# One exp over two score units, one PSUM bank for each pair of heads, three query buffers, and a new order of the steps

## The chip, the cores and the metric

The kernel runs on one core of one Trainium2 chip. Times are device microseconds of one execution; the time that counts is the median over several executions. Engines are named as in the profile: PE is TensorE (matmuls; PEld its weight loads), DVE is VectorE, ACT is ScalarE, POOL is GpSimd, SP is SyncE, which here issues nearly all DMAs.

## What is computed

The reference is attention with a soft cap on the scores, followed by a Fourier mixing block and a feed-forward block, all in fp32. Batch 4, 12 heads, 448 tokens, head size 64, so the model width is 768 and the hidden width 3072.

```python
scores = cap * np.tanh((q @ k.T / 8) / cap)
attn = exp(scores - max); attn = attn / (sum(attn) + 1e-9)
x = attn @ v                                   # heads side by side: (4, 448, 768)
u = x + real(fft(fft(x, axis=1), axis=2))
un = (u - mean(u)) / sqrt(var(u) + 1e-6)       # over the 768 features
out = u + relu(un @ w_ch1) @ w_ch2
```

## The kernel before, in words

**Attention.** The 48 heads are taken as 24 pairs, and two pairs make a group of four heads with 14 weighing units (numbered u) in 7 score units (numbered t, 84 in all, two weighing units each). A weighing unit is a tile of 128 keys of one head against all 448 queries; since 448 is three and a half tiles, the last 64 keys of heads share a tile, the unit in the middle of a group. `scores(t)` (L402) makes eight matmul instructions on 64x64 quadrants of PE into a PSUM tile `s` of two banks (two such tiles); `tanh(t)` (L418) reads them into an SBUF tile `a` of 2 x 448 columns (five such tiles), and `exp(t)` (L422) works on that tile in place. `weigh(u)` (L428) multiplies the weights with V, to which a column of ones is attached, so that the sums of the softmax come out as one more column; it accumulates a pair of heads in one PSUM tile `av` of two banks, one head in each bank, and there is one such tile (`bufs=1`). When a pair is complete, `denominators(p)` (L459) and `normalise(p)` (L469) on DVE read it: an add of the guard, a reciprocal, a memset and four multiplications (L477) into `u`, the tile of one batch.

**Mixing.** For each batch DVE folds tokens and features (L496, L502, L511 to L515), PE makes two stages of matmuls (`stage1` L533, `stage2` L561), ACT and DVE combine between them (L549, L553), DVE adds to `u` (L581, L585), takes mean and variance, and standardises (L637; on ACT for the last batch, L635). PE transposes the result (`u_cols` L644) and ACT copies it into the accumulator `xc`. `operand` and `operand_rest` split it into a leading fp32r part and a rest; `residual` (L768) scales and adds a row of `dev` or `mean`.

**Feed-forward.** 12 groups of two hidden tiles; for each batch `up` (L770) makes 36 matmuls of 128x448 into `ph`, ACT takes the relu (L789), DVE its rest (L790), and `down` (L793) makes 36 matmuls, six in each of six PSUM groups, which DVE adds to `xc` (L821). Groups with an odd `dc` use a bank of the tag `d`; those with an even one use bank 0 or 1 of a two-bank tile of the tag `av`, which is taken anew where `dc` is a multiple of 4. In the first of the 12 groups `down_first` (L828) fills the first two PSUM groups side by side, by hidden tile, adds both (L845), and hands on its two-bank tile, so that `dc` = 2 goes on in bank 1 of it. The fp64 weights are split on DVE and ACT: a half chunk is one `fetch` and three `weights` steps of nine operations (L693 to L725).

**What sets the order.** Nothing is scheduled by a compiler: `ORDER` gives each step a place by hand, the steps are sorted by it, and each engine takes its instructions strictly in that order. An engine whose next instruction waits for a semaphore holds all that stands behind it, and so does SP with its DMAs. `needs` only asserts that the order is possible. All steps up to the last `tanh` run with two `s` tiles; after it their four banks become `ph` banks, so no feed-forward matmul can come before the last `tanh`. PSUM has eight banks: `s` four (later `ph`), `av` two, `d` two.

Of the kernel before, what the change touches and what calls it, by code (L numbers as in the profile page):

```python
# [19 lines left out]
P = 128  # L20
# [38 lines left out]
GF = 2  # L59

# [5 lines left out]
PAD = 16, 16  # L66
# [24 lines left out]
    [(("q", 4), ("q", 4))] * 2 + [(("k", 3), ("k", 3))] + ["x1"] * 3,  # L91
# [10 lines left out]
        268, 267, 275, 302, 488, 487, 523, 524, 710, 727, 693, 702, 841, 846, 843, 850  # L102
    ],
    "combine": [
        237, 243, 238, 249, 436, 437, 449, 452, 649, 670, 659, 673, 830, 832, 826, 831
    ],
    "denominators": [
        44, 75, 104, 124, 155, 187, 216, 248, 286, 319, 342, 378, 426, 465, 504, 534, 566, 594, 641,
        686, 717, 748, 776, 793
    ],  # L110
    "exp": [
# [5 lines left out]
    ],  # L117
    "fetch": [
        8, 32, 43, 79, 145, 222, 299, 388, 479, 834, 854, 893, 921, 948
    ],  # L120
    "fold_features": [
        214, 228, 210, 223, 415, 419, 395, 407, 629, 637, 627, 634, 813, 815, 809, 811
    ],
    "fold_tokens": [
        149, 168, 186, 164, 196, 194, 261, 287, 367, 336, 382, 386, 498, 592, 554, 557, 607, 608, 698,
        749, 775, 767, 803, 804
    ],
    "guards": [
        6
    ],  # L130
    "load_constant": [
        133, 110, 66, 212
    ],
    "load_k": [
        0, 28, 50, 37, 91, 106, 128, 161, 177, 245, 258, 264, 315, 376, 372, 438, 494, 477, 515, 581,
        590, 650, 699, 737
    ],
    "load_q": [
        1, 15, 11, 25, 49, 59, 80, 76, 115, 152, 165, 176, 202, 213, 234, 280, 262, 308, 334, 348, 359,
        397, 402, 433, 490, 503, 502, 548, 539, 570, 632, 666, 646, 704, 725, 736  # L140
    ],
    "load_v": [
# [3 lines left out]
    ],  # L146
    "mirror": [
        199, 203, 387, 393, 609, 619, 805, 806
    ],
    "moments": [  # L150
        273, 312, 307, 311, 495, 510, 544, 532, 729, 733, 759, 762, 852, 855, 853, 856
    ],
    "normalise": [
        46, 82, 109, 127, 157, 190, 219, 251, 290, 321, 343, 381, 431, 470, 514, 541, 569, 600, 647,
        690, 722, 751, 777, 798
    ],
    "operand": [
        421, 425, 453, 454, 442, 507, 695, 639, 677, 715, 678, 799, 848, 816, 828, 900, 901, 906, 909,
        923, 916, 907, 920, 927
    ],  # L160
    "operand_rest": [
        458, 430, 486, 469, 456, 537, 720, 652, 680, 723, 763, 833, 886, 822, 887, 902, 910, 911, 912,
        929, 925, 938, 937, 941
    ],
    "product": [
# [3 lines left out]
    ],  # L169
    "residual": [  # L170
        605, 642, 800, 837, 866, 897, 932, 919, 934, 956, 953, 963
    ],
    "row": [
        584, 752, 908, 946
    ],
    "rows": [
        341, 561, 783, 867
    ],
    "rows_cols": [
        346, 564, 794, 875  # L180
    ],
    "rows_copy": [
        355, 598, 795, 880
    ],
    "rows_out": [
        405, 418, 466, 416, 621, 661, 657, 675, 810, 861, 840, 851, 888, 922, 928, 939
    ],
    "scales": [
        4
    ],  # L190
    "scores": [
# [5 lines left out]
    ],  # L197
    "stage1": [
        233, 242, 236, 246, 434, 435, 443, 446, 640, 658, 651, 664, 827, 829, 824, 821
    ],  # L200
    "stage2": [
        259, 254, 269, 291, 473, 472, 505, 511, 709, 716, 684, 687, 838, 845, 839, 849
    ],
    "standardise": [
        363, 354, 347, 368, 567, 576, 583, 580, 790, 789, 791, 786, 876, 879, 883, 874
    ],
    "tanh": [
# [17 lines left out]
    "weigh": [
# [9 lines left out]
    ],  # L235
# [44 lines left out]
def attention_fft_ffn(  # L280
# [63 lines left out]
    nc.gpsimd.memset(vt[:, :, :, :1], 1.0)  # L344
# [77 lines left out]
    def exp(t):  # L422
        nc.scalar.activation(a_t[t], a_t[t], AF.Exp, scale=capt)  # L423
# [643 lines left out]
```

## Time and profile before

| | us |
|---|---|
| three runs | 910.24, 911.3, 913.85 (median 911.3) |
| the profiled execution | 913.63 |
| its span, first to last instruction | 910.8 |
| PE busy in the span | 892.0 |
| DVE busy | 728.4 |
| ACT busy | 327.1 |
| first and last `av` matmul | 10.7 and 195.8 |

The granted clock of PE is at its full level in the whole span. The page is one execution as the hardware profiler took it. A busy time is the share of a stretch that the instructions of an engine cover; PE's matmuls overlap and their ends are modelled, so a busy PE can still have slack inside. Behind a group of instructions the page gives the idle time just before them and what ended it. The chain of waits goes back from the last instruction, at each step to what released it.

### The profile page before, as it was taken

How to read it: one execution, taken by the hardware profiler on the slowest of the kernel's cores; microseconds unless marked ns; L12 is line 12 of the kernel's file. 1: busy time of each engine (PE TensorE's matmuls, PEld its weight loads, DVE VectorE, ACT ScalarE, POOL GpSimd, SP SyncE). 2: the span in 40 equal slices, each digit the busy share in tenths (PEclk: the TensorE clock that was granted, in tenths of full speed). 3: DMA queues.
4: the chain of work that ended last, by engine and by line, in shares of the span. 5: the costliest groups of instructions: out<-in, count | busy, mean ns of one | idle time of the engine just before them, and what ended most of it. 6: DMA issues, size and time to landing. Idle time of an engine off the chain costs nothing.

```text
span 910.8 us, 17992 instructions
## 1 busy us (share of the span) xinstructions
PE 892.0 (98%) x7452; PEld 784.8 (86%) x7452; DVE 728.4 (80%) x1540; ACT 327.1 (36%) x503; POOL 9.7 (1%) x19
## 2 busy tenths in 40 slices
PE   8899999999989999999999999999999999999998
PEld 4566676778889999999999999999999999999998
DVE  4689999999889787878878788787787877878633
ACT  7989999961502212122221221212212221222200
POOL 0000001000000000000000000000000000000000
PEclk9999999999999999999999999999999999999999
DMA  7653535210202121211212211111211111221033
GB/s 212 172 139 104 135 91 164 66 47 1 74 4 84 53 63 55 72 59 53 63 53 63 65 57 53 53 53 53 67 57 53 53 52 53 54 68 53 18 120 123
DMA packets 50465, 66.60 MB, mean 73 GB/s; under 512 B 25408, under 2 KB 36560, under 8 KB 50384
## 3 DMA queue, kind: packets, MB, share of 16 engines
q1 hardware_dynamic: 50096, 65.13, 24.6%
q8 instruction: 58, 0.95, 0.4%
q10 hardware_dynamic: 288, 0.33, 0.1%
q14 instruction: 23, 0.19, 0.1%
HBM read 59.92 MB, written 5.52 MB: 72 GB/s over the span
## 4 chain that ended last, share of the span: by engine, by line
PE 90%; DVE 7%; issue 1%; ACT 1%; POOL 0%; DVEq 0%; POOLq 0%
PE po L813 37%; PE ph L778 37%; PE av L439 7%; PE s L410 6%; PE pq L561 2%; DVE u L477 1%; PE yps L533 1%; DVE xc L768 1%; DVE tf L502 1%; DVE tf L496 1%; DVE ff L515 0%; DVE y L553 0%; PE warm L351 0%; DVE xs L329 0%; PE pt L644 0%
## 5 line engine op out<-in xcount | busy, mean ns | idle before, releaser
L778 PE MATMUL ph<-xs,w 128*128 128x448 f32 x1728 | 353.3, 362 | 0.0
L813 PE MATMUL po<-hh,w 128*128 128x448 f32 (+1 forms) x1686 | 343.7, 362 | 3.6 <-DVE xc L845 3.6
L778 PEld LDWEIGHTS ph<-xs,w 128*128 128x128 f32 x1728 | 323.4, 187 | 21.9 <-issue 0.3
L813 PEld LDWEIGHTS po<-hh,w 128*128 128x128 f32 x1686 | 314.3, 187 | 27.1 <-DVE xc L845 5.1
L821 DVE TENSOR_TENSOR xc<-xc,po 128x448 f32<-128x448 f32 (+1 forms) x281 | 172.2, 616 | 40.3 <-PE po L813 40.2
L790 DVE SCALAR_TENSOR_TENSOR hh<-ph,hh 128x448 fp32r<-128x448 f32 x96 | 59.9, 624 | 87.3 <-ACT hh L789 86.6
L691 ACT ACTIVATE wt<-raw 128x384 f32<-128x384 f32 x84 | 46.6, 555 | 230.5 <-DVE w L725 230.5
L789 ACT ACTIVATE hh<-ph 128x448 fp32r<-128x448 f32 x96 | 52.3, 544 | 187.1 <-PE ph L778 187.1
L439 PEld LDWEIGHTS av<-vt,a 128*64 128x64 f32 (+1 forms) x2688 | 76.7, 137 | 33.7 <-issue 17.2
L439 PE MATMUL av<-vt,a 128*64 128x65 f32 (+1 forms) x2688 | 82.5, 223 | 8.0 <-issue 3.7
L420 ACT ACTIVATE a<-s,tscale 128x896 f32<-128x896 f32 x84 | 82.5, 1005 | 11.8 <-PE s L410 9.7
L324 ACT CAST w<-wt 128x384 fp32r<-128x384 f32 x84 | 42.8, 510 | 117.8 <-DVE wt L700 117.8
L423 ACT ACTIVATE a<-a,capt 128x896 f32<-128x896 f32 x84 | 83.6, 1039 | 0.4
L410 PE MATMUL s<-q,k 64*64 64x448 f32 x672 | 78.5, 560 | 1.5 <-ACT a L420 1.5
L700 DVE SCALAR_TENSOR_TENSOR wt<-wt 128x384 f32<-128x384 f32 x96 | 53.6, 558 | 9.2
L697 DVE SCALAR_TENSOR_TENSOR wt<-raw,wt 128x384 uint32<-128x384 uint32 x96 | 53.7, 559 | 3.3
L725 DVE TENSOR_TENSOR w<-wt 128x384 fp32r<-128x384 f32 x96 | 53.6, 558 | 3.3
L719 DVE SCALAR_TENSOR_TENSOR wt<-raw,wt 128x384 f32<-128x384 uint32 x96 | 53.5, 557 | 2.9
L329 DVE TENSOR_TENSOR wt<-wt,w 128x384 f32<-128x384 f32 x96 | 52.8, 550 | 0.0
L410 PEld LDWEIGHTS s<-q,k 64*64 64x64 f32 x672 | 23.0, 134 | 21.4 <-issue 9.6
L694 DVE TENSOR_SCALAR wt<-raw 128x384 uint32<-128x384 uint32 x96 | 34.1, 355 | 1.1
L716 DVE TENSOR_SCALAR wt<-wt 128x384 uint32<-128x384 uint32 x96 | 33.9, 354 | 0.5
(65 smaller groups left out, 367.7 us busy)
## 6 DMA issues: line engine op xcount, KB each, us to landing
raw<-w2r SPq DMA_DIRECT2D x48, 384.0 KB
raw<-w1r SPq DMA_DIRECT2D x48, 384.0 KB
q<-qr SPq DMA_DIRECT2D x35, 224.5 KB
outT<-xc SPq DMA_DIRECT2D x23, 224.0 KB
k<-kr SPq DMA_DIRECT2D x12, 256.0 KB
vt<-vr SPq DMA_DIRECT2D x24, 128.0 KB
vt<-vr SPq DMA_DIRECT2D x24, 96.0 KB
k<-kr SPq DMA_DIRECT2D x12, 192.0 KB
```

Of the source, the lines that this page charges most:

```text
L410: nc.tensor.matmul(ps_t[t][h * D : (h + 1) * D, n, :SQ], kt[q, k][rows, k0, h], qk[q, x][rows, :SQ], start=True, stop=True,)
L420: nc.scalar.activation(a_t[t], ps_t.pop(t)[:, :, :SQ], AF.Tanh, scale=tscale)
L423: nc.scalar.activation(a_t[t], a_t[t], AF.Exp, scale=capt)
L439: nc.tensor.matmul(pa_t[p][half * D : (half + 1) * D, j, g * (D + 1) : g * (D + 1) + w], a_t[t][rows, n, q : q + D], vt[rows, p % 2].rearr ...
L697: nc.vector.scalar_tensor_tensor(tu, hi.bitcast(U32), 0xC0000000, tu, op0=ALU.bitwise_and, op1=ALU.bitwise_or)
L700: nc.vector.scalar_tensor_tensor(t, w, HI_MIN, t, op0=ALU.is_ge, op1=mul)
L719: nc.vector.scalar_tensor_tensor(w, lo, 2.0**-52, w, op0=mul, op1=mul)
L725: nc.vector.tensor_tensor(ws[c][1][:, sl], t, w, op=add)
L778: nc.tensor.matmul(ph[:, :S], w_[:, dc * P : (dc + 1) * P], x_, start=(k_ == 0), stop=(k_ == 3 * NDC - 1),)
L790: nc.vector.scalar_tensor_tensor(hh[:, 1], ph[:, :S], 0.0, f32(hh[:, 0]), op0=ALU.max, op1=sub)
L813: nc.tensor.matmul(po[:, q0:q1], w_[:, dc * P : (dc + 1) * P], hh[:, x_, q0:q1], start=(k_ == 0), stop=(k_ == 3 * GF - 1),)
L821: nc.vector.tensor_tensor(ac[:, q0:q1], ac[:, q0:q1], po[:, q0:q1], op=add)
```

## The change

Two score units of `tanh` go into the two halves of one `a` tile of 4 x 448 columns, and one `exp` works on all of it; there are three such tiles instead of five of half the size, and the feed-forward's `hh` uses them likewise, one for a batch. Each pair of heads gets a PSUM tile `av` of one bank, with its seven blocks of 65 columns behind one another, and two such tiles take turns. The tail units in the middle of a group now hold one head of each pair, not two heads of one pair, so that pair p + 1 is begun (its bank taken) one unit before pair p ends. The column of ones stands behind V, not in front. The q of a group comes in two loads instead of three, into three buffers instead of four. In the feed-forward even `dc` take the one-bank `av` tiles in turn. `yh` has one buffer, the padding is larger, loads of V wait for fewer units, and all of `ORDER` is new: 917 steps instead of 971 (42 exps and 12 q loads fewer). The host lays out q, k and v accordingly. The core of the diff, with the lists of `ORDER` cut:

```diff
+ABUFS = 3
...
-PAD = 16, 16
+PAD = 24, 16
...
-    [(("q", 4), ("q", 4))] * 2 + [(("k", 3), ("k", 3))] + ["x1"] * 3,
+    [(("q", 3), ("q", 3)), (("q", 3), ("k", 3)), (("k", 3), ("k", 3))] + ["x1"] * 3,
...
     "exp": [
-        16, 17, 26, 31, 38, 56, 61, 69, 74, 85, 92, 107, 108, 111, 126, 130, 138, 140, 150, 162, 171,
...
+        19, 31, 55, 63, 84, 88, 108, 117, 132, 143, 158, 176, 192, 200, 231, 257, 264, 278, 298, 310,
...
     "tanh": [
-        7, 12, 18, 21, 33, 35, 48, 57, 54, 71, 73, 89, 93, 103, 120, 123, 131, 132, 146, 159, 147, 160,
...
-        735, 758, 772, 764, 781
+        8, 9, 16, 21, 22, 37, 43, 58, 62, 71, 73, 86, 87, 97, 103, 111, 113, 124, 125, 138, 142, 155,
...
+        690, 691, 708, 710, 718
     ],
...
     "weights": [
-        9, 24, 27, 40, 67, 84, 87, 96, 97, 113, 122, 141, 180, 230, 235, 326, 349, 380, 422, 444, 445,
-        556, 586, 648, 663, 689, 825, 872, 878, 894, 915, 930, 940, 944, 947, 950, 959, 962, 964, 966,
-        968, 970
+        36, 38, 39, 41, 49, 54, 65, 70, 78, 92, 106, 116, 134, 160, 162, 208, 226, 241, 341, 394, 405,
+        413, 558, 610, 624, 779, 802, 825, 833, 860, 871, 885, 889, 895, 901, 906, 907, 909, 911, 912,
+        915, 916
     ],
...
     "residual": [
-        605, 642, 800, 837, 866, 897, 932, 919, 934, 956, 953, 963
+        588, 645, 539, 706, 816, 849, 872, 862, 881, 899, 892, 903
...
-    nc.gpsimd.memset(vt[:, :, :, :1], 1.0)
+    nc.gpsimd.memset(vt[:, :, :, D:], 1.0)
...
-        qk[q, i] = new([P, SQ + 1], F32, "q", 4, "q")
-        (nc.scalar if q == 0 and i == 0 else nc.sync).dma_start(qk[q, i], qr[q, i])
+        qk[q, i] = new([P, SQ + 1], F32, "q", 3, "q")
+        (nc.scalar if q == 0 and i == 0 else nc.sync).dma_start(qk[q, i], qr[q, i // 2])
...
-        nc.sync.dma_start(vt[:, p % 2, n0:n1, 1:], vr[p // NP, PAIRS[p % NP], :, n0:n1])
+        nc.sync.dma_start(vt[:, p % 2, n0:n1, :D], vr[p // NP, p % NP, :, n0:n1])
...
-                x = (2 * n if n == h else 1) if i == 3 else 2 * (i > 3)
+                x = 2 * (h if i == 3 else i > 3)
...
-        a_t[t] = new([P, 2, SQ], F32, "a", 5, "a")
-        nc.scalar.activation(a_t[t], ps_t.pop(t)[:, :, :SQ], AF.Tanh, scale=tscale)
-
-    def exp(t):
-        nc.scalar.activation(a_t[t], a_t[t], AF.Exp, scale=capt)
+        if t % 2 == 0:
+            a_t[t // 2] = new([P, 4, SQ], F32, "a", ABUFS, "a")
+        nc.scalar.activation(a_t[t // 2][:, t % 2 * 2 : t % 2 * 2 + 2], ps_t.pop(t)[:, :, :SQ], AF.Tanh, scale=tscale)
+
+    def exp(m):
+        nc.scalar.activation(a_t[m], a_t[m], AF.Exp, scale=capt)
...
     def weigh(u):
         t, n = divmod(u, 2)
         p, head, c = chunk(u)
-        if u % NC == 0:
-            pa_t[p] = psum.tile([P, 2, 512], F32, tag="av", bufs=1, name="av")
-        i = 6 if head is None else 2 * c + head
-        first, last = ((0, 1), (6, 6)) if p % 2 == 0 else ((0, 0), (6, 6))
-
-        def tile(j, g, half, rows, n, i):
+        if u % (2 * NC) in (0, NC - 1):
+            pa_t[u // NC + (u % NC > 0)] = psum.tile([P, 512], F32, tag="av", name="av")
+
+        def tile(p, j, g, half, rows, n, i, start):
+            block = 3 * j + g if g < 3 else 6
             q = (2 * g + half) * D if g < 3 else 6 * D
-            w = D + 1 + int(g == 2 and c == 0 and half != j)
             nc.tensor.matmul(
-                pa_t[p][half * D : (half + 1) * D, j, g * (D + 1) : g * (D + 1) + w],
-                a_t[t][rows, n, q : q + D],
-                vt[rows, p % 2].rearrange("k n c -> k (n c)")[:, i * (D + 1) : i * (D + 1) + w],
-                start=u % NC == first[j] and g == 0,
-                stop=u % NC == last[j] and g == 3,
+                pa_t[p][half * D : (half + 1) * D, block * (D + 1) : (block + 1) * (D + 1)],
+                a_t[t // 2][rows, t % 2 * 2 + n, q : q + D],
+                vt[rows, n if i == NC - 1 else p % 2, i],
+                start=start,
+                stop=False,
                 skip_group_check=True,
             )
 
+        if head is None:
+            p -= p % 2
+            for g in range(3):
+                for h in range(2):
+                    for half in range(2):
+                        tile(p + h, n, g, half, slice(h * D, (h + 1) * D), n, NC - 1, h == 1 and n == g == 0)
+            if n == 1:
+                for j in range(2):
+                    for h in range(2):
+                        tile(p + h, j, 3, j, slice(h * D, (h + 1) * D), j, NC - 1, False)
+            return
         for g in range(3):
-            for j in (0, 1) if head is None else (head,):
-                rows = slice(P) if head is not None else slice(j * D, (j + 1) * D)
-                for half in range(2):
-                    tile(j, g, half, rows, n, i)
-        for j in range(2):
-            if head is None:
-                tile(j, 3, j, slice(j * D, (j + 1) * D), n, i)
-            elif head == 1:
-                tile(j, 3, j, slice(P), n - 1 + j, i - 1 + j)
+            for half in range(2):
+                tile(p, head, g, half, slice(P), n, 2 * c + head, u % (2 * NC) == g == 0)
+        if head == 1:
+            for j in range(2):
+                tile(p, j, 3, j, slice(P), n - 1 + j, 2 * c + j, False)
 
     def denominators(p):
         b = p // NP
         if b not in u_t:
             u_t[b] = new([P, 4, DM], F32, f"x{b % 2}", 1, "u")
             nc.gpsimd.memset(u_t[b][FOLD:, 3], 0.0)
-        pa = pa_t[p][:, :, : 4 * (D + 1)].rearrange("q j (g c) -> q j g c", g=4)
-        den = den_t[p] = new([P, 2, 4, 1], F32, "den", 2, "den")
-        nc.vector.tensor_scalar_add(den, pa[:, :, :, :1], guard)
+        pa = pa_t[p][:, : 7 * (D + 1)].rearrange("q (i c) -> q i c", i=7)
+        den = den_t[p] = new([P, 7, 1], F32, "den", 2, "den")
+        nc.vector.tensor_scalar_add(den, pa[:, :, D:], guard)
         nc.vector.reciprocal(den, den)
 
     def normalise(p):
         b, c0 = p // NP, PAIRS[p % NP] * 2 * D
-        pa = pa_t[p][:, :, : 4 * (D + 1)].rearrange("q j (g c) -> q j g c", g=4)[..., 1:]
+        pa = pa_t[p][:, : 7 * (D + 1)].rearrange("q (i c) -> q i c", i=7)[:, :, :D]
         den = den_t[p]
         u = u_t[b][:, :, c0 : c0 + 2 * D].rearrange("q g (j c) -> q j g c", j=2)
 
-        def part(out, rows, j, g):
-            x = pa[rows, j, g]
-            nc.vector.tensor_tensor(out, x, den[rows, j, g].to_broadcast(x.shape), op=mul)
-
-        part(u[D:FOLD, :, 3], slice(FOLD, P), slice(2), 2)
-        nc.vector.memset(den[FOLD:, :, 2], 0.0)
+        def part(out, rows, i):
+            x = pa[rows, i]
+            nc.vector.tensor_tensor(out, x, den[rows, i].to_broadcast(x.shape), op=mul)
+
+        part(u[D:FOLD, :, 3], slice(FOLD, P), slice(2, 6, 3))
+        nc.vector.memset(den[FOLD:, 2:6:3], 0.0)
         for j in range(2):
-            part(u[:D, j, 3], slice(j * D, (j + 1) * D), j, 3)
-        part(u[:, :, :3], slice(P), slice(2), slice(3))
+            part(u[:D, j, 3], slice(j * D, (j + 1) * D), 6)
+        nc.vector.tensor_tensor(
+            u[:, :, :3],
+            pa[:, :6].rearrange("q (j g) c -> q j g c", j=2),
+            den[:, :6].rearrange("q (j g) c -> q j g c", j=2).to_broadcast([P, 2, 3, D]),
+            op=mul,
+        )
...
-        half = new([P, 2, NK], F32, "yh", 2, "yh")[:FW]
+        half = new([P, 2, NK], F32, "yh", 1, "yh")[:FW]
...
-            hh = hs[b, n] = new([P, 2, S], F32R, "a", 5, "hh")
+            if n == 0:
+                hs[b] = new([P, GF, 2, S], F32R, "a", ABUFS, "hh")
+            hh = hs[b][:, n]
...
-            if dc % 2:
-                po = psum.tile([P, 512], F32, tag="d", name="po")
-            else:
-                if dc % 4 == 0:
-                    both = psum.tile([P, 2, 512], F32, tag="av", bufs=1, name="po")
-                po = both[:, dc % 4 // 2]
+            po = psum.tile([P, 512], F32, tag=("av", "d")[dc % 2], name="po")
...
-        both = psum.tile([P, 2, 512], F32, tag="av", bufs=1, name="po")
-        po = both[:, 0], psum.tile([P, 512], F32, tag="d", name="po")
+        po = [psum.tile([P, 512], F32, tag=tag, name="po") for tag in ("av", "d")]
...
-            at(load_v, p, i, needs=[("weigh", u) for u in units(p - 2)])
+            at(load_v, p, i, needs=[("weigh", 7 * p - 8 + n) for n in range(2 - p % 2)] if p > 1 else [])
...
-        at(tanh, t, needs=[("scores", t), ("scales",)])
-        at(exp, t, needs=[("tanh", t)])
+        at(tanh, t, needs=[("scores", t), ("scales",)] + [("tanh", t - 1)] * (t % 2))
+        if t % 2:
+            at(exp, t // 2, needs=[("tanh", t - 1), ("tanh", t)])
...
-                at(denominators, p, needs=[("weigh", 7 * p + 6), ("guards",)] + ([("denominators", p - 1)] if p else []))
+                at(denominators, p, needs=[("weigh", 7 * p + 7 - p % 2), ("guards",)] + ([("denominators", p - 1)] if p else []))
...
```

## Rows read from the trace of the kernel before

**Rows 1.** The page: busy time of PE, and the chain that ended last by engine.
```profile
PE 892.0 (98%) x7452; PEld 784.8 (86%) x7452; DVE 728.4 (80%) x1540; ACT 327.1 (36%) x503; POOL 9.7 (1%) x19
...
PE 90%; DVE 7%; issue 1%; ACT 1%; POOL 0%; DVEq 0%; POOLq 0%
```
**Rows 2.** Stretches: busy PE, PEld, DVE, ACT, POOL (instructions), clock, DMA share, GB/s.
```profile
20.00:40.00 20.00, 17.75 (x381) 11.08 (x375) 13.34 (x40) 19.03 (x21) 0.00 (x0) 1.00 0.52 139
40.00:60.00 20.00, 18.02 (x415) 12.49 (x414) 12.93 (x32) 17.01 (x20) 0.00 (x0) 1.00 0.58 164
60.00:80.00 20.00, 19.46 (x408) 14.73 (x404) 18.08 (x48) 16.51 (x21) 0.00 (x0) 1.00 0.32 91
...
120.00:140.00 20.00, 19.57 (x414) 13.69 (x416) 19.17 (x51) 19.19 (x21) 0.70 (x1) 1.00 0.40 106
...
190.00:200.00 10.00, 8.62 (x179) 7.25 (x172) 9.20 (x29) 6.40 (x9) 0.79 (x1) 1.00 0.19 49
...
220.00:300.00 80.00, 77.03 (x402) 70.26 (x399) 71.45 (x148) 23.50 (x44) 1.27 (x2) 1.00 0.17 49
300.00:600.00 300.00, 300.00 (x1501) 280.94 (x1500) 247.10 (x474) 63.95 (x125) 0.00 (x0) 1.00 0.20 58
```
**Rows 3.** The tile av: its matmuls, ns min/median/max, first and last start in us.
```profile
L439 PE MATMUL av<-vt,a x2688: 213/222/272, 10.7 to 195.8; 128*64 128x65 f32 x144, 64*64 64x65 f32 x48
```
**Rows 4.** The chain in order of time: start, us, what.
```profile
34.24 3.32 PE av L439 x112
...
37.59 0.24 DVE den L466
...
39.02 0.57 DVE u L477
...
39.84 1.04 PE av L439 x28
40.88 1.66 PE s L410 x16
```
**Rows 5.** Who waited for whom: us in total, times, longest.
```profile
PEld av L439 <- DVE u L477: 4.0, 5, 0.9
...
PE po L813 <- DVE xc L845: 3.6, 4, 1.4
...
PE av L439 <- DVE u L477: 1.8, 3, 0.6
```
**Rows 6.** The page's groups: busy, mean ns of one, idle before and what ended it.
```profile
L420 ACT ACTIVATE a<-s,tscale 128x896 f32<-128x896 f32 x84 | 82.5, 1005 | 11.8 <-PE s L410 9.7
...
L423 ACT ACTIVATE a<-a,capt 128x896 f32<-128x896 f32 x84 | 83.6, 1039 | 0.4
...
L700 DVE SCALAR_TENSOR_TENSOR wt<-wt 128x384 f32<-128x384 f32 x96 | 53.6, 558 | 9.2
...
L694 DVE TENSOR_SCALAR wt<-raw 128x384 uint32<-128x384 uint32 x96 | 34.1, 355 | 1.1
```
**Rows 7.** Timeline around the third batch's first down groups: start, us, what, idle before.
```profile
250.33 2.08 DVE L768 TENSOR_TENSOR xc<-xc,dev 128x896 f32<-128x896 f32 x2
252.33 1.14 DVE L845 TENSOR_TENSOR xc<-xc,po 128x448 f32<-128x448 f32 x2
253.00 3.28 PE L813 MATMUL po<-hh,w 128*128 128x448 f32 x15 [1.43 <-DVE xc L845]
```
**Rows 8.** Timeline of ACT from 40 us.
```profile
40.32 1.97 ACT L423 ACTIVATE a<-a,capt 128x896 f32<-128x896 f32 x2
```
**Rows 9.** Groups by form in 0:230: two copies by ACT of different lengths.
```profile
L324 ACT COPY xc<-pt 128x448 f32<-128x448 f32 x17 | 9.1, 548 | 2.7 <-PE pt L644 2.7
...
L324 ACT COPY yh<-yps 97x256 f32<-97x256 f32 x16 | 5.9, 375 | 8.4 <-PE yps L533 6.4 <-DVE y L553 1.7 <-ACT a L423 0.2
```
**Rows 10.** Timeline of the start.
```profile
9.64 1.96 ACT L423 ACTIVATE a<-a,capt 128x896 f32<-128x896 f32 x2
...
10.72 1.50 PE L439 MATMUL av<-vt,a 128*64 128x65 f32 x40
```

More of the change, by code (lines that the diff above doesn't have):

```diff
@@ L109 @@
-        686, 717, 748, 776, 793
+        51, 74, 101, 133, 152, 172, 217, 230, 280, 305, 331, 354, 411, 438, 476, 498, 542, 552, 609,
+        631, 676, 704, 730, 742
     ],
     "exp": [
[5 rows of a table removed]
+        19, 31, 55, 63, 84, 88, 108, 117, 132, 143, 158, 176, 192, 200, 231, 257, 264, 278, 298, 310,
+        325, 342, 363, 402, 427, 446, 453, 471, 489, 508, 519, 537, 553, 579, 604, 630, 655, 675, 683,
+        698, 711, 721
     ],
     "fetch": [
-        8, 32, 43, 79, 145, 222, 299, 388, 479, 834, 854, 893, 921, 948
+        5, 30, 48, 76, 107, 147, 295, 313, 532, 761, 811, 886, 896, 904
@@ L120 @@
     ],
     "fold_features": [
-        214, 228, 210, 223, 415, 419, 395, 407, 629, 637, 627, 634, 813, 815, 809, 811
+        205, 206, 195, 204, 387, 392, 380, 384, 594, 605, 581, 584, 753, 755, 750, 752
     ],
     "fold_tokens": [
-        149, 168, 186, 164, 196, 194, 261, 287, 367, 336, 382, 386, 498, 592, 554, 557, 607, 608, 698,
-        749, 775, 767, 803, 804
+        120, 139, 146, 148, 178, 187, 242, 303, 323, 357, 364, 367, 465, 470, 518, 545, 561, 560, 707,
+        709, 719, 728, 744, 745
@@ L150 @@
[L150 to L164, printed above, removed]
@@ L165 @@
-    "product": [
[3 rows of a table removed]
-    ],
-    "residual": [
-        605, 642, 800, 837, 866, 897, 932, 919, 934, 956, 953, 963
[L172 to L190, printed above, removed]
-    "scores": [
[5 rows of a table removed]
+        12
+    ],
@@ new lines @@
+    "load_constant": [
+        115, 42, 197, 46
+    ],
+    "load_k": [
+        0, 14, 3, 28, 69, 109, 141, 156, 193, 233, 216, 260, 317, 334, 373, 389, 451, 490, 493, 527,
+        576, 601, 642, 656
+    ],
+    "load_q": [
+        2, 10, 23, 34, 80, 98, 128, 166, 184, 196, 263, 276, 308, 336, 368, 406, 445, 474, 511, 520,
+        566, 626, 659, 664
+    ],
+    "load_v": [
[3 rows of a table added]
+    ],
+    "mirror": [
+        188, 191, 378, 379, 571, 573, 746, 748
+    ],
+    "moments": [
+        253, 286, 283, 294, 456, 469, 500, 492, 667, 700, 687, 672, 795, 798, 799, 800
+    ],
@@ new lines @@
+    "normalise": [
+        60, 83, 123, 136, 169, 177, 225, 236, 296, 311, 337, 361, 426, 442, 482, 507, 547, 557, 612,
+        648, 694, 712, 737, 743
+    ],
+    "operand": [
+        459, 393, 454, 408, 409, 418, 621, 575, 732, 643, 703, 740, 767, 823, 801, 841, 844, 843, 837,
+        845, 866, 879, 857, 867
+    ],
+    "operand_rest": [
+        499, 397, 563, 509, 419, 436, 628, 615, 772, 774, 768, 765, 777, 850, 854, 851, 855, 856, 883,
+        875, 877, 884, 876, 887
+    ],
+    "product": [
[3 rows of a table added]
+    ],
@@ L197 @@
+    "residual": [
+        588, 645, 539, 706, 816, 849, 872, 862, 881, 899, 892, 903
+    ],
+    "row": [
+        477, 679, 842, 870
+    ],
+    "rows": [
+        309, 512, 713, 808
+    ],
+    "rows_cols": [
+        319, 534, 722, 819
+    ],
+    "rows_copy": [
+        332, 554, 727, 821
+    ],
+    "rows_out": [
+        344, 390, 374, 399, 556, 646, 591, 637, 747, 820, 813, 810, 846, 865, 859, 848
+    ],
+    "scales": [
+        6
+    ],
+    "scores": [
[5 rows of a table added]
     ],
     "stage1": [
-        233, 242, 236, 246, 434, 435, 443, 446, 640, 658, 651, 664, 827, 829, 824, 821
+        209, 232, 211, 220, 401, 404, 412, 424, 608, 619, 607, 627, 769, 764, 770, 775
@@ L216 @@
-        889, 891, 896, 892, 899
+        355, 358, 365, 366, 391, 388, 549, 562, 572, 574, 583, 599, 741, 739, 759, 760, 792, 796, 829,
+        830, 834, 835, 832, 839
     ],
     "u_copy": [
-        385, 390, 401, 412, 424, 428, 610, 614, 622, 625, 631, 636, 801, 807, 817, 819, 865, 873, 885,
-        890, 895, 898, 904, 905
+        356, 359, 376, 381, 395, 396, 565, 568, 578, 589, 602, 606, 749, 751, 762, 766, 797, 807, 831,
+        836, 838, 840, 847, 853
     ],
     "warmup": [
-        2
+        1
@@ L793, in down @@
     def down(g, b):
-        both = yield from down_first(b) if g == 0 else ()
+        if g == 0:
+            yield from down_first(b)
         for dc in range(2 * (g == 0), NDC):
-            if dc % 2:
-                po = psum.tile([P, 512], F32, tag="d", name="po")
-            else:
-                if dc % 4 == 0:
-                    both = psum.tile([P, 2, 512], F32, tag="av", bufs=1, name="po")
-                po = both[:, dc % 4 // 2]
+            po = psum.tile([P, 512], F32, tag=("av", "d")[dc % 2], name="po")
             ac = xc[b, dc // 2][:, dc % 2]
@@ L846, in down_first @@
             yield
-        return both
     def pieces():
@@ L899, in prepare @@
         for i in range(2):
-            at(load_v, p, i, needs=[("weigh", u) for u in units(p - 2)])
+            at(load_v, p, i, needs=[("weigh", 7 * p - 8 + n) for n in range(2 - p % 2)] if p > 1 else [])
             if p % 2 == 0:
-                for x in (0,) if i == 0 else (1, 2):
-                    t0, t1 = ((0, 4), (3, 4), (3, 7))[x]
+                x = 2 * i
+                if 1:
+                    t0, t1 = ((0, 4), (), (3, 7))[x]
                     at(load_q, p // 2, x, needs=[("scores", 7 * (p // 2 - 1) + t) for t in range(t0, t1)] if p else [])
@@ L909, in attend @@
         pairs = sorted({u // 7 for u in (2 * t, 2 * t + 1)})
-        at(scores, t, needs=[("load_q", t // NC, x) for x in ((0, 1, 2) if t % NC == 3 else (2 * (t % NC > 3),))] + [("load_k", t // NC, int(t % NC >= KT[1]))])
-        at(tanh, t, needs=[("scores", t), ("scales",)])
-        at(exp, t, needs=[("tanh", t)])
+        at(scores, t, needs=[("tanh", t - 2)] * (t > 1) + [("load_q", t // NC, x) for x in ((0, 2) if t % NC == 3 else (2 * (t % NC > 3),))] + [("load_k", t // NC, int(t % NC >= KT[1]))])
+        at(tanh, t, needs=[("scores", t), ("scales",)] + [("tanh", t - 1)] * (t % 2))
+        if t % 2:
+            at(exp, t // 2, needs=[("tanh", t - 1), ("tanh", t)])
         for u in (2 * t, 2 * t + 1):
-            at(weigh, u, needs=[("exp", t), ("load_v", u // NC, int((6 if chunk(u)[1] is None else 2 * chunk(u)[2] + chunk(u)[1]) >= KT[1]))] + ([("weigh", u - 1)] if u else []))
+            at(weigh, u, needs=[("exp", t // 2), ("load_v", u // NC, int((6 if chunk(u)[1] is None else 2 * chunk(u)[2] + chunk(u)[1]) >= KT[1]))] + ([("weigh", u - 1)] if u else []))
         for p in range(B * NP):
             if 7 * p + 6 in (2 * t, 2 * t + 1):
-                at(denominators, p, needs=[("weigh", 7 * p + 6), ("guards",)] + ([("denominators", p - 1)] if p else []))
+                at(denominators, p, needs=[("weigh", 7 * p + 7 - p % 2), ("guards",)] + ([("denominators", p - 1)] if p else []))
                 at(normalise, p, needs=[("denominators", p)])
```

40 lines of the change are left out of this document (11 added, 29 removed), and 50 rows, old and new, of the table ORDER.

## The prediction

> **What bounds the kernel now.** I read the page's first part, then the busy times of each engine by stretch, the chain of waits, the waits in total, and at four places the timeline. TensorE is busy for 892.0 of 910.8 us and makes 90% of the chain, VectorE 7% [rows 1]. So whatever the change gains must come out of the 18.8 us in which TensorE stands, or out of slack hidden inside its bursts; its work does not shrink, since the numbers of score, `av` and feed-forward matmuls stay as they are. The reader is to see where the 18.8 us lie [rows 2]: 2.25 us in 20:40, 1.98 in 40:60, 0.54 in 60:80, 0.43 in 120:140, 1.38 in 190:200, 2.97 in 220:300, and none in 300:600; the rest is at the start, at the end and in the stretches between. From 300 us on nothing of this change can help. The attention stage, where `av` runs from 10.7 to 195.8 us [rows 3], is close to a balance of three engines: before 60 us ScalarE is nearly full (19.03 of 20 us in 20:40) and VectorE half empty (13.34 and 12.93 of 20); from 60 us on VectorE takes over (18.08, then 19.17 of 20 in 120:140) [rows 2]. So early idle time of VectorE that the new order fills with later work is worth something, and early time of ScalarE too.
>
> **The change part by part**, against the profiled execution (913.63 us, of which 910.8 are span and 2.83 lie around it).
>
> *Two one-bank `av` tiles, attention.* Now a pair's first `av` matmul waits for the whole normalisation of the pair before it, since both use the only `av` tile. The chain shows one such place: 112 `av` matmuls, then VectorE from 37.59 to 39.59, then `av` again at 39.84 [rows 4]: 2.3 us, in which TensorE had only two score units left to fill in. By the totals such waits cost TensorE 1.8 us at matmuls and 4.0 us at weight loads [rows 5]; and because a pair's matmuls come bunched behind the wait, scores come late, and `tanh` waited 9.7 us for them in all [rows 6]. After the change a bank is written again only six weighing units after its pair is complete; at 2688/168 = 16 matmuls a unit [rows 3] and 3.32/112 = 0.030 us each [rows 4], that is 2.8 us of `av` alone, and some 5 us with the scores between. A 2.0 us normalisation fits unless VectorE has over 3 us queued ahead of it, which from 60 us on it can have. Bounds 0 and -4.0; I take -2.5, nearer to the larger end, since the first three places lie where VectorE is half empty.
>
> *The same banks in the feed-forward.* Today `down_first` fills bank 0 of the double tile and a `d` bank; the next group (dc = 2) writes bank 1 of the same tile and yet starts only when the first sum of L845 has been read: two residuals hold VectorE first, L845 starts at 252.33, takes half of 1.14, and L813 starts at 253.00 after 1.43 us idle [rows 7]. There are four such places, one for each batch, 3.6 us in total [rows 5], which is nearly all of TensorE's idle time in 220:300 [rows 2] and some before. With separate banks the group doesn't share a tile with what L845 reads. What is late next is dc = 4, which takes the bank back two groups later (12 matmuls, 2.4 us at the 0.2 us each of 300:600 [rows 2]), and both L845 together take 1.14 us, so that wait should find its sum read. Bounds 0 and -3.6; I take -3.3, the rest for VectorE being 71.45 of 80 us busy in 220:300 and so sometimes late elsewhere.
>
> *One exp over two units.* 84 calls become 42. Two exps back to back take 1.97 us where one takes 1.039 [rows 6, 8]: the second costs 0.93 us. If that is all streaming, the merged call saves nothing. A copy of 256 elements takes 375 ns and one of 448 takes 548 [rows 9], 0.90 ns an element, by which 896 elements stream for 0.81 us and 0.12 us are fixed: 42 x 0.12 = 5.0 us. I take 0.1 us a call, near that end, as the copies are the only rows that separate the two. It counts only where ScalarE binds, before 60 us, with some 13 merged calls (ScalarE has 41 instructions in 20:60 [rows 2], half of them exps, and about six exps before), so -1.0 us after some loss (bounds 0 and -5.0).
> "Perfetto Trace Analysis" of the Trainium skill, section Optimizing Scalar/DVE Operations, puts the fixed busy time of a ScalarE instruction on SBUF at about 93 ns, by which the merge would free an estimated 42 x 0.093 = 3.9 us of ScalarE; the trace has no exp of 1792 elements to show it.
>
> *What the merge delays.* The first weighing starts at 10.72 us, right after the first of two exps begun at 9.64 [rows 10]. In the new order three tanh go ahead of the first exp, which lasts twice as long: start about 10.6, end 12.5. TensorE gets two more score units in that time (16 matmuls take 1.66 us [rows 4]), so 1.9 us late turns into about 0.3 lost; bounds 0 and +1.9, I take +0.5. Behind a weighing that waits for exp all later matmuls queue, so in each of the 42 steps TensorE can stand while the longer exp ends: two score units take 1.66 us, the merged exp about 1.87, so up to 0.21 us a step, 8.8 us. But the order puts two more tanh between an exp and the weighing of the one before, and from 60 us on transform matmuls lie between. Bounds 0 and +8.8; I take +1.0.
>
> *New order.* Of the 42 early conversion steps, 26 stood ahead of the last tanh before and 25 do after; but numbers 13 to 17 (from 0) move from places 230 to 380 of 781 to places 160 to 241 of 718. A half chunk is three steps with five operations of 0.56 and four of 0.355 us [rows 6], 4.2 us, so 5 steps are about 7 us of VectorE work that leave the stretch in which it is full for one in which it stood (13.7 us idle in 20:60 [rows 2]). Two residuals more go ahead, of 1.04 us each [rows 7], and one conversion step less (1.4 us), which leaves some 6 us. Bounds -7 and +2 (the residuals come ahead of something that TensorE waits for); I take -2.2, a third, because TensorE is nearly full in the same stretch and can't follow further.
>
> *At nothing.* A third fewer q loads with three buffers instead of four: the DMA share is 0.52 in 20:40 and 0.32 in 60:80 [rows 2], so they are hidden; the next q is asked for three to four score units ahead, and if that cover failed each group would lose a load of 1 to 2 us at the head of the scores. Loads wait in SyncE's queue with the raw weights behind them, which nothing needs at once. The ones column at the end of a V row, seven reciprocals instead of eight and one `yh` buffer leave the same instructions. The padding shifts all addresses: if the 0.2 us of a feed-forward matmul [rows 2] moved by half a per cent, 3456 of them would make 3.5 us either way; I take 0.
>
> Sum: -2.5 - 3.3 - 1.0 + 0.5 + 1.0 - 2.2 = -7.5 us, so 906.1 for an execution like the profiled one. That one lies 2.3 us above the median of the runs (911.3), so the forecast for a median is **903.8 us**.
>
> **The rivals.**
> *A, VectorE takes it back.* The matmuls that no longer wait for normalise run ahead into others that need VectorE (folds, y, residual, operand rests), and the stage ends when VectorE's queue does. For it: 19.17 of 20 us in 120:140 and 7% of the chain. Against it: the four feed-forward places are plain TensorE waits. Left over are half of the -3.3 and -0.5 before: about -2, 909.
> *B, the long exp paces TensorE: slower.* The 0.21 us are lost in nearly every one of the 42 steps, +8.8, and the early -1.0 and the order's -2.2 don't come since each engine waits for the other in turn; the `av` banks bring nothing as the wait for exp stands in place of normalise; with -3.3 in the feed-forward and +0.5 at the start the sum is +6.0: 917. It decides from about 37 of the 42 on (37 x 0.21 - 2.8 = +5, half a per cent). Against it: from 60 us on ScalarE has time to run ahead (16.51 of 20 us busy in 60:80).
> The same section of "Perfetto Trace Analysis" says that where ScalarE isn't saturated but causes bubbles on other engines, breaking its instructions up can finish work sooner: that speaks against the merge, and is this rival; how the trace bears on it stands in the sentence before.
> *C, TensorE closes up.* Nearly all idle time of 10:200 goes (6.6 us in the stretches of rows 2; I estimate 9 with those between) beside the 3.6: -12.5, 899, and below it if bursts tighten too.
>
> **How the numbers follow.** Forecast 0.50 (its own range 900 to 907), A 0.21, B 0.12, C 0.17. Half a per cent, about what a measurement tells from no change, is 4.6 us: faster is below 906.7, slower above 915.9. Faster: C, and nine tenths of the forecast, 0.62; slower: most of B, 0.10; the rest, 0.28, within. The range for 8 in 10 runs from 895 (part of C, addresses helping) to 913 (A with the start's loss).
>
> **What would show it.** The waits of L813 for L845 are gone or under 0.5 us; waits of `av` for L477 are gone; the merged exp's mean is near 1.9 us (0.1 below twice 1.039 less the overlap); the first `av` starts near 12.5 us; the last before 192. The feed-forward's 0.2 us a matmul stays. It is wrong if TensorE's idle time in 60:200 grows behind L423's successor, or if 300:880 changes length.

## The result and the profile after

The changed kernel takes **903.83 us** (median of four runs, 901.73 to 905.32) against 911.26 us for the kernel before, measured beside it (910.24 to 913.85): a ratio of 0.9913, interval 0.9884 to 0.9941. The same kernel, timed again later, gave 903.19 us, 0.9910 [0.9896, 0.9923]. The forecast was 903.8 us. The profiled execution took 903.83 us with a span of 902.0. Of the eight executions of these two measurements four have a mean granted clock of 0.998 (903.83 to 905.32 us), as the profiled one has, and four of 1.000 (901.73 to 903.83).

The page's first part and the chain by engine, against [rows 1]:
```profile
PE 889.0 (99%) x7452; PEld 783.0 (87%) x7452; DVE 729.2 (81%) x1540; ACT 319.1 (35%) x461; POOL 9.2 (1%) x19
...
PE 93%; DVE 3%; ACT 2%; DMA 1%; issue 0%; SPq 0%; POOL 0%; POOLq 0%
```
VectorE's share of the chain fell from 7 to 3%; a DMA has come into it. The stretches of [rows 2], in the same columns, and two short ones between 36 and 42.4 us:
```profile
20.00:40.00 20.00, 17.68 (x380) 10.94 (x376) 16.52 (x47) 18.97 (x16) 0.00 (x0) 0.98 0.60 168
40.00:60.00 20.00, 20.00 (x440) 12.52 (x434) 12.83 (x34) 16.76 (x14) 0.00 (x0) 0.93 0.46 130
...
220.00:300.00 80.00, 80.00 (x410) 73.91 (x409) 75.77 (x154) 25.49 (x48) 1.67 (x2) 1.00 0.18 53
300.00:600.00 300.00, 300.00 (x1501) 281.19 (x1500) 246.32 (x470) 64.31 (x125) 0.00 (x0) 1.00 0.20 58
...
36.00:39.20 3.20, 1.07 (x32) 0.93 (x28) 3.05 (x9) 2.97 (x3) 0.00 (x0) 1.00 1.01 281
39.20:42.40 3.20, 3.20 (x20) 0.80 (x16) 0.51 (x1) 0.00 (x0) 0.00 (x0) 0.51 0.36 136
```
220:300 is full now (77.03 before), 300:600 is the same to the matmul. But 20:40 is no better than before: 2.13 us of what is missing is one wait, and behind it TensorE's granted clock stood at half (0.51, the level of 1.2 GHz), which a full busy share hides and the clock column shows. The chain through that place, in order of time:
```profile
31.26 0.43 SPq L395
...
31.74 0.65 SPq L372
...
32.44 5.71 DMA vt<-vr
...
38.27 1.04 PE av L437 x28
39.31 3.19 PE s L409 x16
42.51 2.86 PE av L437 x112
```
The V load of the fifth pair stands in SP's queue behind a K load (L395) and the feature constants (L372), shares the DMA engines with a raw weight chunk and with these two, and lands 5.7 us after its issue. The 16 score matmuls behind the wait take 3.19 us instead of the 1.66 of [rows 4].

The tile `av`, against [rows 3] and [rows 5]:
```profile
L437 PE MATMUL av<-vt,a x2688: 217/222/368, 11.2 to 190.6; 128*64 128x65 f32 x144, 64*64 64x65 f32 x48
...
PEld av L437 <- DVE u L482: 0.7, 1, 0.7
```
The last `av` starts 5.2 us earlier than before, of which 0.9 us lie ahead of the first `tanh` (it starts at 6.4 us in this execution and at 7.3 in the one before); from there to the end of the span 711.4 us remain, 3.6 less than the 715.0 before. Of the waits for normalise (4.0 us at weight loads, 1.8 at matmuls) 0.7 is left, and no `po` matmul waits for L853, the new number of L845. The two groups of [rows 6] that changed, and ScalarE's timeline at the start:
```profile
L420 ACT ACTIVATE a<-s,tscale 128x896 f32<-128x896 f32 x84 | 82.0, 1013 | 18.3 <-PE s L409 17.1
...
L423 ACT ACTIVATE a<-a,capt 128x1792 f32<-128x1792 f32 x42 | 75.5, 1801 | 0.5
```
```profile
9.41 1.78 ACT L423 ACTIVATE a<-a,capt 128x1792 f32<-128x1792 f32 x1
11.09 1.89 ACT L420 ACTIVATE a<-s,tscale 128x896 f32<-128x896 f32 x2
```
The merged exp lasts 1.80 us, but the next instruction starts 1.68 us after it (11.09 - 9.41): the ends overlap, as in [rows 8], where the second of two took 1.97 - 1.039 = 0.93. So a pair of units costs 1.68 instead of 2 x 0.93: 0.18 us saved per merge, 7.6 us in 42, and ScalarE's busy time fell by 8.0. ScalarE has not become the faster for it: `tanh` now waits 17.1 us for scores, 9.7 before.

### The profile page after: what moved, and what is told of

It is laid out like the page before. It is cut to its first block, busy times and chain, and to the rows that moved or that the text cites. A ratio compares the mean times of both kernels' runs of the same rounds, so it can differ in the third digit from the quotient of the medians.

```text
span 902.0 us, 17850 instructions
## 1 busy us (share of the span) xinstructions
PE 889.0 (99%) x7452; PEld 783.0 (87%) x7452; DVE 729.2 (81%) x1540; ACT 319.1 (35%) x461; POOL 9.2 (1%) x19
## 4 chain that ended last, share of the span: by engine, by line
PE 93%; DVE 3%; ACT 2%; DMA 1%; issue 0%; SPq 0%; POOL 0%; POOLq 0%
PE ph L788 38%; PE po L821 37%; PE av L437 6%; PE s L409 6%; PE pq L571 2%; PE yps L543 1%; PE po L843 1%; PE pt L654 1%; ACT a L423 1%; ACT a L420 1%; DMA vt<-vr 1%; DVE y L563 1%; DMA k<-kr 0%; PE warm L350 0%; DVE xs L328 0%
## 5 line engine op out<-in xcount | busy, mean ns | idle before, releaser
L420 ACT ACTIVATE a<-s,tscale 128x896 f32<-128x896 f32 x84 | 82.0, 1013 | 18.3 <-PE s L409 17.1
L423 ACT ACTIVATE a<-a,capt 128x1792 f32<-128x1792 f32 x42 | 75.5, 1801 | 0.5
L729 DVE SCALAR_TENSOR_TENSOR wt<-raw,wt 128x384 f32<-128x384 uint32 x96 | 53.5, 557 | 2.9
L409 PEld LDWEIGHTS s<-q,k 64*64 64x64 f32 x672 | 20.7, 134 | 21.9 <-issue 10.3
```

The source lines that it names most:

```text
L409: nc.tensor.matmul(ps_t[t][h * D : (h + 1) * D, n, :SQ], kt[q, k][rows, k0, h], qk[q, x][rows, :SQ], start=True, stop=True,)
L420: nc.scalar.activation(a_t[t // 2][:, t % 2 * 2 : t % 2 * 2 + 2], ps_t.pop(t)[:, :, :SQ], AF.Tanh, scale=tscale)
L423: nc.scalar.activation(a_t[m], a_t[m], AF.Exp, scale=capt)
L729: nc.vector.scalar_tensor_tensor(w, lo, 2.0**-52, w, op0=mul, op1=mul)
```

## The experiments

The runs of one group share their comparison runs of the kernel before; each ratio is to these.

**One suspected loss: the late V load** (the changed kernel, one place of `load_v`).
```diff
-        13, 32, 18, 24, 52, 53, 77, 79, 121, 102, 135, 127, 159, 180, 199, 201, 215, 254, 235, 261, 289,
+        13, 32, 18, 24, 52, 53, 77, 79, 101, 102, 135, 127, 159, 180, 199, 201, 215, 254, 235, 261, 289,
```


> The changed kernel with one load moved: the first load of V of the fifth pair goes from place 121 to 101 of the order, ahead of the fetch of raw weights, a load of K and featT, behind which it landed 5.7 us after its issue; at 36.2 us TensorE stood 2.13 us for it and then had its half clock from 39.3 to 42.7 us. Theory: the wait and the half clock both go, and the time falls by about 2.1 + 1.5 = 3.6 us in executions that have the half clock, about 2 in those that don't, so the median goes to 900.5 to 902. Rival (ScalarE binds there, or the loads behind become late instead): the wait goes or moves, the time stays within 1 us.

901.05 us (900.45 to 902.56), ratio 0.9886 [0.9871, 0.9901]. Its stretches, columns as above:
```profile
20.00:40.00 20.00, 20.00 (x434) 12.52 (x434) 16.21 (x48) 19.80 (x17) 0.00 (x0) 1.00 0.57 154
40.00:60.00 20.00, 20.00 (x476) 13.89 (x476) 16.17 (x42) 18.94 (x19) 0.00 (x0) 1.00 0.56 162
```
Wait and half clock are gone.

**The same once more, and the feature constants moved behind the loads.**


> The changed kernel with the V load of the fifth pair early, once more, beside the other two on one chip. Theory: 901.1 us, 2 to 3 us below the changed kernel. The rival, that the first run owed its 901.05 us to an early start of the full clock: 903 us.

899.95 us, 0.9872 [0.9858, 0.9887]: the gain comes again. Shown: this one late load costs the change 2.1 to 3.9 us (903.19 and 903.83 against 901.05 and 899.95). With `load_constant` 0 at 137 instead of 115 besides:

> The changed kernel with the V load early, and with the load of the feature constants moved from 115 to 137, behind the K and V loads of the fifth pair. If the K load too is held up by what stands before it in SyncE's queue, its wait of about 0.6 us goes and the time is 900.3 to 900.7 us. The rival: the fifth pair waits for nothing that costs by now, and the time is that of the early V load, 901.0 us, within its interval.

900.38 us, 0.9883 [0.9865, 0.9901]. The waits of PE for K, first with the early V load alone, then with the constants moved besides:
```profile
PE s L409 <- DMA k<-kr: 1.5, 1, 1.5
```
```profile
PE s L409 <- DMA k<-kr: 0.4, 1, 0.4
```
Both waits lie near 87 us and are for another K load, issued at 82 us. For the K load of the fifth pair, near 36 us, TensorE waits in neither profile (it is busy for all of 20:40 in both), so the edit had no wait there to take away. The time lies in the 900.3 to 900.7 us of the theory, but the early V load alone, measured beside it, took 899.95: the rival holds, the fifth pair waits for nothing that costs by now.

**The banks in the feed-forward, undone and alone.** Undone: in the first of the 12 groups `dc` = 2 goes on in the bank that `down_first` fills first. (Before, it was the other bank of the same tile; here the bank itself is shared, so that the wait for its reader must come back.)
```diff
...
-            po = psum.tile([P, 512], F32, tag=("av", "d")[dc % 2], name="po")
+            if g == 0 and dc == 2:
+                po = first
+            else:
+                po = psum.tile([P, 512], F32, tag=("av", "d")[dc % 2], name="po")
...
```


> The changed kernel, but in the first feed-forward group dc = 2 goes on in the bank that dc = 0 has just used, so that it must wait until the first sum (L845 before) has been read; nothing else is different. Theory: the four waits of 3.6 us in all that this read cost before are a plain loss, because no other wait stands behind them; they come back at the same four places and the time rises by 3 to 4 us, to about 907.4. Rival (VectorE ends the stage anyway, so the waits are only shown at another place): the four waits come back but the time rises by less than 1 us.

905.5 us (903.6 to 909.85), 0.9938 [0.9919, 0.9958]: 1.7 to 2.3 us above the two medians of the changed kernel, with intervals that overlap, and less than the 3 to 4 us expected. The waits for the sum (here L854) are back, at two places of the four, and PE is busy for 77.47 of the 80 us in 220:300 (80.00 in the changed kernel):
```profile
PE po L823 <- DVE xc L854: 2.4, 2, 1.4
```
Alone: the kernel before, with only this group's `dc` = 2 in a free bank of `ph`.
```diff
+            if (g, dc) == (0, 2):
+                po = stage["up"].tile([P, 512], F32, tag="ph", name="po")
```


> The kernel before with one edit: in the first feed-forward group dc = 2 takes a bank of the tag ph instead of bank 1 of the double tile, so that it shares no tile with what L845 reads. Theory: the four waits of 3.6 us in all go, nothing stands behind them, and the time falls by 2.5 to 3.6 us, to about 908.3. Rival (VectorE ends that stretch, 71 of 80 us busy): the waits go, other waits take their place in 220:300, and the time stays within 1 us.

907.05 us (906.74 to 907.67), 0.9954 [0.9940, 0.9967]: 4.2 us faster, more than the 2.5 to 3.6 expected. PE is busy for 2.9 us more in 220:300 and 0.65 us more in 200:220 (20.00, 19.35 before), the stretches of the four waits:
```profile
220.00:300.00 80.00, 79.94 (x413) 73.47 (x412) 74.58 (x154) 25.02 (x47) 1.27 (x2) 1.00 0.18 51
```
So in this kernel a tile of two banks is waited for as a whole: the matmul group in one bank waited for the reading of the other, and in a tile of its own it doesn't. The waits are worth 1.7 to 2.3 us (put back) and 4.2 us (taken away alone).

**All the banks, in the old order.** The kernel before with one-bank `av` tiles in turn, in both stages, the tails regrouped as in the change; `exp`, q loads and all other places stay, but for the denominators and V loads of even pairs, which must come a unit later.
```diff
-        if u % NC == 0:
-            pa_t[p] = psum.tile([P, 2, 512], F32, tag="av", bufs=1, name="av")
+        if u % (2 * NC) in (0, NC - 1):
+            pa_t[u // NC + (u % NC > 0)] = psum.tile([P, 512], F32, tag="av", name="av")
...
```


> The kernel before with the banks alone: one-bank av tiles in turn, in attention and feed-forward, with the tail units grouped as in the change (which they need); 84 single exps, five a tiles, three q loads, and the old order, in which only the denominators and normalisations of even pairs and the loads of V that follow them stand a little later. Theory: 3.6 us in the feed-forward and 2.5 in the attention stage, so about 905.3 against 911.3; the waits of av for L477 are gone. Rival (the attention stage's gain is the new order's): only the 3.6 us come, 907.7, and the last av starts near 195.8 as before.

914.87 us (914.39 to 914.96), 1.0034 [1.0021, 1.0047]: **slower than before**, which neither theory had. Its waits of PE (engine and line waited for, us in total, times, longest), and one of the places in PE's timeline; `yps` and `pq` are the two matmul stages of the mixing, `rt` the transposed statistics, `pt` the transposed result:
```profile
PE rt L634 <- DVE stat L629: 4.7, 3, 3.2
PE yps L553 <- DVE y L573: 2.7, 2, 1.8
...
PE yps L553 <- DVE ff L535: 1.8, 1, 1.8
PE pt L664 <- DVE u L657: 1.4, 1, 1.4
```
```profile
143.31 0.43 PE L634 MATMUL rt<-ident,stat 128*8 128x128 f32 x2 [3.17 <-DVE stat L629]
143.67 3.27 PE L420 MATMUL s<-q,k 64*64 64x448 f32 x16
```
The 42nd and 63rd `tanh` start at 90.9 and 139.1 us, 3.1 and 2.9 ahead of the kernel before (94.0, 142.0). Having run ahead, TensorE reaches its mixing matmuls earlier than VectorE has their inputs, stands 3.2 us at one of them, and goes on at half clock (the 16 score matmuls behind it take 3.27 us); the 84th `tanh` comes 3.7 us behind, and the first feed-forward matmul starts at 202.2 us against 196.7 before. That is rival A, in a kernel that has no new order.

**The same with six mixing steps of three kinds moved later**, as far as the attention had run ahead: the transposes of the statistics (`rt`, 346 to 351.3 and 564 to 576), two combinations behind the first stage (243 to 247.8, 249 to 252.8) and two first stages (242 to 247.5, 246 to 252.5).

> The kernel with the one-bank tiles alone and the old order, but with the places of the residual and statistics steps (346 to 351.3, 564 to 576), of the statistics' combination (243 to 247.8, 249 to 252.8) and of the first stage behind it (242 to 247.5, 246 to 252.5) moved later, as far as the attention now runs ahead. If the banks alone lost because TensorE reached the transform of the residual while VectorE still had its statistics to do (3.2 us of waiting at 140 to 143, then a halved clock), most of that goes and the time is 909 to 911 us. The rival: VectorE's own work ends the stage whatever the places, and the time stays within 1 us of 914.9.

911.3 us (909.81 to 912.22), 0.9994 [0.9986, 1.0002]: 3.6 us won back, 0.3 us short of what the theory gave, and still no gain on the kernel before, though the feed-forward's waits are gone in it. The stand of 3.2 us is down to 0.6. Its waits of PE:
```profile
PE yps L553 <- DVE y L573: 2.4, 3, 1.8
...
PE yps L553 <- DVE ff L535: 1.8, 1, 1.8
PE rt L634 <- DVE stat L629: 1.6, 3, 0.6
PE pt L664 <- DVE u L657: 1.6, 2, 1.4
PE pt L664 <- DVE rowt L640: 1.3, 1, 1.3
PE pq L581 <- DVE y L573: 1.1, 1, 1.1
```
9.8 us of such waits; in the changed kernel two of this kind are left (`pq` and `po` for DVE), 0.9 us. The time in which PE stands (stretch less its busy time):

| | 10:60 | 60:190 | 190:220 | 220:300 |
|---|---|---|---|---|
| before | 5.1 | 3.1 | 2.0 | 3.0 |
| banks, old order | 2.3 | 10.4 | 2.7 | 0.0 |
| banks, some steps later | 3.0 | 7.7 | 2.9 | 0.0 |
| changed | 3.0 | 2.6 | 0.5 | 0.0 |
| changed, V early | 0.8 | 3.0 | 0.5 | 0.0 |

**The merge alone.** The changed kernel, each exp in two halves (84 calls again).
```diff
-        nc.scalar.activation(a_t[m], a_t[m], AF.Exp, scale=capt)
+        for i in range(2):
+            a = a_t[m][:, 2 * i : 2 * i + 2]
+            nc.scalar.activation(a, a, AF.Exp, scale=capt)
```


> The changed kernel with each exp of 128x1792 made as two of 128x896, back to back, at the same place in the order. The merged call lasts 1.79 us and the next instruction starts 1.68 us after it, where two single ones took 1.87, so the split adds 42 x 0.19 = 7.8 us of ScalarE. Theory: ScalarE binds only before 60 us, so 1 to 2 us of it show (about 905.3), in 0:60. Rival 1 (the merge is the gain of the attention stage): +5 us and more, about 909. Rival 2 (the long exp makes TensorE wait, so that splitting helps, since the first two weighing units can start 0.9 us earlier): 1 us faster or more, about 902.8.

904.13 us (901.32 to 907.0), 0.9917 [0.9897, 0.9936]: no difference, but not a clean one. In its profile TensorE stands at the same matmul of the fifth pair (at 38.45 us), for 1.5 us instead of 2.1, and at the full clock afterwards:
```profile
PE av L439 <- DVE u L484: 1.5, 1, 1.5
```
The profile puts this wait down to the normalisation of another pair, but the trace has the V load landing at 38.32 us, 0.13 us ahead of the matmul, as in the changed kernel (38.14 and 38.27): it is the late V load again. The next expectation takes it for gone, which is wrong. So again with the early V load:

> The kernel with the early load of V (901.05) and, beside that, each exp made as two halves back to back. In the changed kernel the split cost nothing (904.13 against 903.83), but there the split also made the load of V come in time: its wait and the half clock were gone. Theory: the merge is worth 2 to 3 us once V is early, since it takes 0.19 us of ScalarE from each of the about 13 exps before 60 us, where ScalarE is full; so about 903.5, with the loss in 0:60 (the 21st tanh about 2 us later than 41.2). Rival (the merge is worth nothing): 901 to 901.5.

901.92 us (901.22 to 902.35), 0.9894 [0.9880, 0.9907], against 901.05 and 899.95 with the merge. By the medians the merge is worth 0.9 to 2.0 us; the intervals overlap, and zero is not excluded. In this profile `av` waits for exp 0.7 us at matmuls, 2.0 with the merge.

**The moved conversion steps.** With the early V load, steps 13 to 17 put late again, with the chunk fetch that they need.
```diff
-        36, 38, 39, 41, 49, 54, 65, 70, 78, 92, 106, 116, 134, 160, 162, 208, 226, 241, 341, 394, 405,
+        36, 38, 39, 41, 49, 54, 65, 70, 78, 92, 106, 116, 134, 211, 216, 300, 321, 340, 341, 394, 405,
...
```


> The kernel with the early load of V, in which five conversion steps (numbers 13 to 17) and one fetch go back to about the share of the stage at which they stood before: places 211 to 340 instead of 160 to 241. Theory (work of VectorE moved into the time when it stood is worth about 2 us): about 903, VectorE less busy before 60 us and later with the transforms of the first two batches. Rival (TensorE is full in the same stretch, the places don't matter): 901 to 901.5.

903.79 us (903.28 to 904.31), 0.9915 [0.9902, 0.9929]: 2.7 us slower than with the early V load alone, but not in the way meant. The 42nd `tanh` starts at 85.8 us, no later than without the edit (86.8); counted from the first `tanh` it is 79.4 us in both. Then, in the chain:
```profile
88.45 0.34 SPq L687
...
88.83 1.48 SPq L395
...
90.36 3.68 DMA q<-qr
...
94.08 1.76 PE s L409 x6
```
A q load stands behind a weight fetch and a K load in SP's queue (the fetch had itself waited for a conversion step, L729, that ends at 88.4 us), lands late, and TensorE waits 2.0 us. What the early conversions bring by filling VectorE's idle time stays open.

## Why the prediction was right, point by point

The total is right to 0.1 us, and that closeness is luck: a loss that the prediction left out (without it the gain is 10 to 11 us, not 7.5) and a gain that it sized too small cancel.

- **The same banks in the feed-forward (-3.3): right.** The waits are gone, -3.6 from the last `av` on in the traces, and 1.7 to 4.2 us by the two experiments.
- **Two one-bank `av` tiles, attention (-2.5): the waits went as described (5.8 to 0.7 us), but the term is not a term by itself.** With the banks and the old order, the stages up to the first feed-forward matmul lose 5.5 us (202.2 against 196.7), more than the 4.2 us that the feed-forward wins. The step that failed is the sum's assumption that the parts add up: -2.5 and -3.3 by it, +3.3 us measured for the two together.
- **New order (-2.2, from idle time of VectorE): right in sign, too small, and its reason not shown.** VectorE does work more in 10:60 (37.6 us busy, 31.3 before), the 6 us that were counted. The larger part seems to be that the mixing steps stand where TensorE now comes by; moving six of them won 3.6 us in the old order, the rest is argued and not shown. Between the banks with some steps later (911.3) and the changed kernel with early V and 84 exps (901.92) lie 9.4 us; what differs is the order, with the q loads, the `a`, `hh` and `yh` tiles, the column of ones and the padding. Of these the order decides when TensorE reaches the places of those 9.8 us of waits; neither it nor the others were tried by themselves.
- **One exp over two units (-1.0): the size of a call was too small** (0.1 us for 0.18, above the prediction's bound of 0.12), the effect on the time near what was forecast (0.9 to 2.0 us by the medians, or nothing). "ScalarE: Activation LUTs" of the Trainium skill, section What ACT_TABLE_LOAD costs, gives 280 ns and 0.833 ns a column for an activation with one pointer operand, with 93 ns of it overlapping the next one. The trace agrees: by this an estimated 1.77 us for 1792 columns (1.80 measured) and 187 ns per call saved (0.18 us measured). The 93 ns that the prediction quotes from "Perfetto Trace Analysis" of the Trainium skill are half of what was measured, and the measurement decides.
- **What the merge delays (+0.5 and +1.0): right in kind.** The first `av` starts at 11.2 us, not 12.5, but the first `tanh` of this execution started 0.9 us earlier as well (6.4, 7.3 before): from `tanh` to `av` it is 4.8 us instead of 3.4. In the two profiles with the early V load, whose first `tanh` starts at 7.3 us, `av` starts at 12.2 and 12.4. Waits for exp at `av` matmuls come to 2.0 us, three times, not 42.
- **At nothing: wrong in one place.** "Loads wait in SyncE's queue with the raw weights behind them, which nothing needs at once": here the weights and constants stand ahead, and a V load that is needed behind them. 2.1 us of waiting and 1.6 of half clock (half of the 3.2 us from 39.2 on) are 3.7 in the trace, 2.1 to 3.9 in the time. For a q load that comes late the prediction puts down 1 to 2 us: the one in the last experiment took 3.7 us to land, and TensorE waited 2.0 us, with half the clock behind it. The padding left the feed-forward as it was: 1501 matmuls in 300:600 in both kernels.
- **Rivals.** A is the mechanism of the banks in the old order. B is refuted: the kernel is not at 917 us, and split exps don't make it faster. C (899) is about what the early V load reaches, 899.95 to 901.05, the fastest version here.

## What to carry to other kernels

Taking away a wait lets an engine reach its next one sooner: price a removed wait together with the places of what comes behind it, since here the same banks cost 0.3% in the old order and belong to a gain of 0.9% in the new one. When an order is rewritten, follow each small load through its queue, and read the clock column beside the busy share. A PSUM tile over two banks was waited for as one here: matmul groups that are read at different times go into tiles of their own.

## What was not expected of the hardware

- **A stand of 2 to 3 us can cost TensorE twice.** After 2.1 us (changed kernel), 2.0 (late q) and 3.2 us (banks, old order) without work the granted clock fell to about its half (0.51 to 0.53 in the stretch behind); in the first and the third the next 16 score matmuls took 3.2 to 3.3 us instead of 1.66. Of the banks in the old order, the stretch behind the stand:
```profile
143.40:147.00 3.60, 3.60 (x34) 1.34 (x36) 0.49 (x1) 0.00 (x0) 0.00 (x0) 0.53 0.00 0
```
  "TensorE: Matmul & The Clock Gate" of the Trainium skill, section HAM oscillation — how this bites in real kernels, tells of matmuls that start at the low clock after a wait for DMA; these traces agree, and show it behind a wait for VectorE too. They also show that it doesn't come each time: with the feed-forward banks undone TensorE stood 2.6 us for the same V load and went on at the full clock, while the changed kernel, timed again, stood 2.6 us there and had half (0.57 in 39.6:43). The first line is that wait, the second the stretch behind it, both with the banks undone:
```profile
PE av L437 <- DMA vt<-vr: 2.6, 1, 2.6
```
```profile
39.30:42.70 3.40, 3.40 (x72) 2.18 (x74) 1.35 (x3) 1.30 (x2) 0.00 (x0) 1.00 0.63 221
```
- **Here a small load cost its place in the queue.** The V load took 5.7 us at a DMA share of 1.01 in 36:39.2; issued 20 places earlier it is waited for by nobody.
